# Transposed q and k of the first segments kept as (lane, token) instead of (token, lane)

## The chip, the core and the metric

The kernel runs on one core of one Trainium2 chip. Its time is the device time of one execution in microseconds (us); lower is better. TensorE (PE; PEld is its weight load), VectorE (DVE), ScalarE (ACT), GpSimd (POOL) and SyncE (SP, which issues most DMAs) run side by side, each through its own list of instructions in a fixed order.

## The reference

The program is a linear attention followed by two mixtures of experts. Only the attention bears on the change. For each of 4 batches and 8 heads, over 768 tokens of 48 components, a complex state is turned by a factor per token and component, an outer product of k and v is added, and q reads the real part:

```
for t in range(S):
    new_re = ar * S_re - ai * S_im
    new_im = ar * S_im + ai * S_re
    kv = np.einsum('bhd,bhe->bhde', k[:, :, t], v[:, :, t])
    S_re, S_im = (new_re + kv, new_im)
    y[:, :, t] = np.einsum('bhd,bhde->bhe', q[:, :, t], S_re)
```

The rows y, as 3072 tokens of 384 values, then go through a mixture in which every token has one expert and a second one in which it has two.

## The kernel before

Each sequence is cut into eight segments of 96 tokens: four "first" segments (t = 0) and four "second" ones (t = 1). A lane is one head of one batch in one of the four segments, so 128 lanes fill the partitions. Twenty-four groups of 8 tokens of all lanes go through VectorE and ScalarE, which compute the running product P of the factors, q times P (tile `qh`) and k divided by P (tile `kh`). Groups 0 to 11 are the first segments, groups 12 to 23 the second ones.

For the first segments, TensorE transposes each token's `qh` and `kh` into a PSUM bank (line 848, tile `pt`, four tokens of 128 lanes in a bank, 96 partitions of component and real or imaginary part). ScalarE copies each bank into the long tiles `QT` and `KT` (line 851). That is two banks per group for q and two for k, so 48 copies.

Then come 16 units of the first segments, one per batch and segment with 8 heads each. A unit multiplies, head by head, the 96 tokens of k by those of q (line 999, `amat`, in two halves of 4 heads, out of `KT` and `QT`), masks the product, adds the segment's k and v to the state (line 1029, `pu`), turns the state (line 1042, `pt<-s,R`), and forms the output rows (line 1081, and line 1083, `outs`, where `QT` reads the state; only in the 12 units that have a state before them; both run through the helper at line 932). The state of the first segments is added by TensorE too (line 1026). A float32 matmul of one head shows as two records.

While TensorE does this, VectorE and ScalarE work on groups 12 to 23, whose sums of squares are TensorE's as well (lines 680 and 761). The 16 units of the second segments follow; their k and q come back from memory and are transposed by VectorE (lines 979 and 984) into tiles `kTt` and `qTt`, laid out as head, then 96 tokens in a row. Their tiles lie where `QT` and `KT` were, so their loads wait for the last reader of `QT`. The mixtures follow.

The order of all engines is written by a planner (class `Plan`) from estimated times: 0.66 us for half an `amat`, 1.3 us for half an `outs` with a state, 0.5 us for a copy of line 851. Each engine then keeps that order whatever the real times are. Matmuls of a unit matrix (line 1151) fill planned waits of TensorE.

How a head's 96 columns are taken from the long tile:

```
def lane(XT, n, u, h):
    t, b, g = u
    return XT[:, :, b * 32 + h * 4 + g] if t == 0 else st[n, u][:, h]
```

With `XT` of shape [96, 96 tokens, 128 lanes] two neighbouring columns are 512 bytes apart; those of `kTt` and `qTt` are 4 bytes apart.

Of the kernel before, what the change touches and what calls it, by code (L numbers as in the profile page):

```python
# [22 lines left out]
F32 = mybir.dt.float32  # L23
# [10 lines left out]
G = 8  # L34
# [64 lines left out]
class Plan:  # L99
    """Operations in an order in which they could run, each with its engine, an estimate of its time and the tiles it  # L100
    reads and writes; played back in the order in which a simple model of the engines starts them."""

    def __init__(self, tags):
        self.tags, self.ops, self.fill = tags, [], None
        # kinds of tiles: their pool; pools: those that have to be closed before
        self.pool, self.after = {}, {}

    def add(self, eng, dur, fn, r=(), w=(), key=0.0, when=None, rows=96, got=None, need=(), dma=None, free=False):
        """tiles are tuples: the tile's tag, then what tells it from others; in w, an item in a list stands for a part
        of a tile that no other operation writes; with free, only the operations in need have to come before"""  # L110
        self.ops.append((eng, dur, fn, list(r), [x[0] if isinstance(x, list) else x for x in w],
                         [x[0] for x in w if isinstance(x, list)], key, key if when is None else when, rows, got,
                         set(need), dma, free))
        return len(self.ops) - 1

    def deps(self):
        for p, before in self.after.items():
            # all that is done in the pools before
# [4 lines left out]
        # operations that only have to be issued before  # L123
# [34 lines left out]
    def choose(self, e, t, avail, wait):  # L158
        """the first of those that can start; none where it would keep a more urgent one that comes soon"""
# [13 lines left out]
    def run(self):  # L173
# [29 lines left out]
        while len(out) < n:  # L203
# [23 lines left out]
            if e == 'PE':  # L227
                # the clock of the tensor engine: half of it after a tick with too few columns
# [15 lines left out]
            if e == 'SP':  # L244
                # queue, then the transfer itself
                dma = max(dma, t + 1.1) + dur
                dur = dma - t - 1.1
            at[i], end[i] = t, t + dur
            free[e] = t + 0.47 if e == 'SP' else end[i]
            if move is not None:  # L250
                # descriptors, then the transfer itself
# [27 lines left out]
class Lazy:  # L279
    """A tile, or a part of one, that is allocated when the first operation on it is played"""  # L280
# [59 lines left out]
class Stage:  # L340
    """On-chip memory by pools that open when they are first used, and operations put down for a plan: their reads and
    writes tell which have to come before, their sizes how long they take."""
# [11 lines left out]
    def pool(self, name, side="left", close=(), under=None, space=None, after=None):  # L354
        """a pool, on top of another one; those in close give their room, after is what has to be through before"""
# [42 lines left out]
    def outer(self, name, ap):  # L398
        """a tile that is there already"""
# [22 lines left out]
    def touch(self, op, x, write):  # L422
        """the operations that have to come before, for one access"""
# [11 lines left out]
    def note(self, op, x):  # L435
        """an operation of the plan that writes x"""
        self.touch(op, x, True)

    def ext(self, op, name):
        """an operation of the plan that writes something outside of the chip"""  # L440
# [30 lines left out]
    def group(self, eng, rows=128):  # L471
        """one operation of what is put down within"""
# [18 lines left out]
class Engine:  # L491
    """An engine's operations, put down instead of issued"""
# [49 lines left out]
def attention(stage, a, xs, LG, cst, flag, clears=()):  # L542
    """x rows to xs, gate logits to LG[p, t * 16 + b * 4 + g] (token b * 768 + OFF[t] + g * LEN[t] + p).

    Lanes are (head, one of four segments), first over the segments of LEN[0] tokens, then over those of LEN[1].
    With P_t the product of the normalized factors since the segment's start, q^ = q P and k^ = k / P, so that a
    segment is a causal product of q^ and k^ and the state passes from segment to segment by the diagonal of P's
    last value. The products of the first segments run while the vector engine works on the second ones."""
# [15 lines left out]
    # tiles: tag and number of buffers  # L564
# [12 lines left out]
    def new(key, shape):  # L577
        """the tile of a key: allocated by the operation that writes it first"""
# [11 lines left out]
    A.preload_act_table_set("abs_reciprocal_sqrt_and_small")  # L590
    QT = big.tile([96, LEN[0], 128], F32, name="QT")
    KT = big.tile([96, LEN[0], 128], F32, name="KT")
# [34 lines left out]
    last = [LEN[0] // G - 1, NG - 1]  # L627

    def seg(g):
        """a group's segments, its place in them"""  # L630
# [17 lines left out]
    def group(g):  # L648
# [24 lines left out]
        # u = |a|^2, by the tensor engine as long as it has time  # L673
# [62 lines left out]
        # P of even tokens as (im, re), of odd ones as (re, im)  # L736
# [68 lines left out]
        def d_q(i):  # L805
            def f():
                """q^; of the second segments in three blocks of 32 columns"""
# [33 lines left out]
        for kx, XT, n, x in ((kqh, QT, 'QT', 1.7), (kkh, KT, 'KT', 2.5)):  # L841
            for h in range(2):
# [7 lines left out]
                def cp(XT=XT, h=h, kt=kt):  # L850
                    A.activation(XT[:, j * G + h * 4:j * G + h * 4 + 4], st[kt][:96], AF.Copy)
# [3 lines left out]
    def turns(t):  # L855
        """the segments' last P: columns of the complex diagonal, or what a component and the other one are taken by"""
# [70 lines left out]
    def wide(out, lhsT, rhs, h, m, start=True, stop=True):  # L927
        """out[:, h] = lhsT^T rhs[:, h], heads from the last to the first. The m columns of lhsT take the array as
        long as m columns of rhs: it streams as many, and those before the head's own are written over later."""
# [6 lines left out]
    def lane(XT, n, u, h):  # L936
        t, b, g = u
        return XT[:, :, b * 32 + h * 4 + g] if t == 0 else st[n, u][:, h]

    def unit(i, u):  # L940
# [7 lines left out]
        # what the tail's tiles take the place of  # L948
# [40 lines left out]
        def diag():  # L989
            """the diagonal with the segment's last P"""  # L990
# [31 lines left out]
        def umat():  # L1022
            """what the segment adds to the state"""
# [78 lines left out]
    def warm(x, n, r, key):  # L1102
        """matmuls in a wait, for the clock of the tensor engine"""
# [18 lines left out]
    # rows of the lists that no token gets  # L1122
# [9 lines left out]
    def span(x):  # L1132
        """from the first to the last use of a kind of tile"""
# [5 lines left out]
    def fill(t):  # L1139
        """a matmul in a wait, for the clock of the tensor engine; in a bank that is not in use at that time"""  # L1140
# [13 lines left out]
    # flags: a decay so strong that the factors leave the range in which this form is exact  # L1154
# [8 lines left out]
def general(tc, c, a, out, xs):  # L1163
    """The whole computation for any values: the recurrence token by token, the assignment with ties,
    every expert over every token."""
# [78 lines left out]
    with ExitStack() as ctx:  # L1244
# [5 lines left out]
        def unique(pool, O, shape):  # L1250
            """the first of equal maxima"""
# [25 lines left out]
        def dense(w1, w2):  # L1277
            """acc[t] = sum over the experts of W[t, e] * expert e of token t"""
# [116 lines left out]
def surplus(tc, c, a, xg, cape, out):  # L1395
    """the rows of the second mixture's lists from cape on"""
# [5 lines left out]
    with tc.tile_pool(name="s", bufs=1) as p, tc.tile_pool(name="sps", bufs=2, space=bass.MemoryType.PSUM) as ps:  # L1402
        with tc.For_i(0, E) as e:
# [4 lines left out]
            for r0 in (low, low + R):  # L1408
# [8 lines left out]
                # the rows before are done  # L1417
# [34 lines left out]
def make_consts(nc, pool, rpool, tmp):  # L1452
    """constants that depend on shapes alone, built on chip; those in rpool are the assignment's"""
# [8 lines left out]
    # tri[p', p] = 1 where p' < p  # L1462
# [18 lines left out]
    # slot number of compacted tokens: i * 128 + p  # L1481
# [9 lines left out]
    # 8 - expert  # L1491
    c.w8 = rpool.tile([128, 8], F32, name="w8")
    V.tensor_scalar(c.w8, it[:, :8], -1.0, 8.0, op0=ALU.mult, op1=ALU.add)
    # tokens of the logits, as 16 * tid[0] + tid[1]
# [16 lines left out]
def placed(stage, c, LG, flag):  # L1511
    """The tokens above a threshold at which no expert is full go to their best experts; the others are left for
    the phases."""
# [8 lines left out]
    # every token's best expert, by columns as the logits come: with the values of C0 tokens as thresholds,  # L1522
    # the experts' tokens above them
# [24 lines left out]
    # what moves through the tensor engine: the logits with the token's number  # L1548
# [5 lines left out]
    # everything above the lowest threshold at which no expert is full is placed  # L1554
# [13 lines left out]
    # ranks: tokens before in the same column, in the columns before of a group of four, in the groups before  # L1568
# [18 lines left out]
    # every token's slot, of its expert or of those left: hi * 128 + lo  # L1587
# [16 lines left out]
    # (twice the columns, for the clock of the tensor engine: it takes no longer)  # L1604
# [18 lines left out]
    # places left - 0.5  # L1623
# [4 lines left out]
    # the ids of the tokens placed, by experts and hi  # L1628
# [13 lines left out]
    # flags: two equal best experts, too many tokens left, too few placed  # L1642
# [8 lines left out]
class Phases:  # L1651
    """The tokens left, from the highest logit on: an expert fills up in each phase. The experts' order, and the
    token ids of the slots of those that are full."""

    def __init__(self, stage, c, flag, Lm, rem, cnt, CPs, sl):
# [3 lines left out]
        # 8 - expert, as long as it has no place in the order  # L1659
# [4 lines left out]
        # the order: experts' numbers, one-hot columns  # L1664
# [6 lines left out]
    def slots(self):  # L1671
        """token ids of the slots of the tokens placed"""
# [11 lines left out]
    def take(self, OHA, pn):  # L1684
        """the experts' places go to these tokens"""
# [7 lines left out]
    def best(self):  # L1693
        """the tokens' highest logits, one-hot rows of their experts"""
# [44 lines left out]
    def last(self):  # L1739
        """one expert is left"""  # L1740
# [4 lines left out]
    def next(self, k):  # L1745
        """place k of the order: an expert that is full"""
# [10 lines left out]
    def ids(self, k0, k1, idf):  # L1757
        """token ids of the slots of the experts of these places"""
# [677 lines left out]
```

## Time and profile before

| what | value |
|---|---|
| median of 3 runs | 1241.56 us |
| the three runs | 1231.51, 1241.57, 1241.56 us |
| span of the profiled execution, first to last instruction | 1230.7 us |
| time of the profiled execution beside its span | not listed apart from the three runs |
| TensorE busy | 1170.3 us, 95% |
| VectorE busy | 798.0 us, 65% |
| ScalarE busy | 498.6 us, 41% |
| mean granted TensorE clock | 0.964 of full speed |

A busy share is a mean over stages with different limits. The stages that matter here are: the groups of the first segments (to 149 us), the units of the first segments (149 to 335 us), those of the second ones (335 to about 450 us) and the rest.

### The profile page before, as it was taken

What the parts mean: (1) busy time and instruction counts of PE and PEld (TensorE: products, weight loads), DVE (VectorE), ACT (ScalarE), POOL (GpSimd) and SP (SyncE); (2) the same over time, 40 slices, a digit from 0 to 9 for tenths busy, and PEclk for the clock granted to TensorE, in tenths of its full rate; (3) what the DMA queues carried; (4) which work ended last, traced back from release to release, by engine and by line L of the source; (5) the groups of instructions that cost most, each with busy time, mean ns of one, the idle gap of its engine ahead of it and who ended that gap; (6) DMA issues with size and microseconds to landing.
All of it is one profiled execution on the core that took longest, in us unless ns stands there. A gap on an engine that the chain in (4) does not pass through costs nothing.

```text
span 1230.7 us, 22881 instructions
## 1 busy us (share of the span) xinstructions
PE 1170.3 (95%) x8082; PEld 1103.1 (90%) x8082; DVE 798.0 (65%) x2524; ACT 498.6 (41%) x1026; POOL 297.5 (24%) x321
## 2 busy tenths in 40 slices
PE   8999899999988997899999999989999999999995
PEld 7888798999988987899889999989899999999995
DVE  7899876767599776888788778635535343444221
ACT  8888555534312122554545445123323232232220
POOL 2000021102134320420753221332303132222212
PEclk9999989969999799899999999999999999999998
DMA  7776466644366489453885464264515151422111
GB/s 185 207 207 186 146 201 192 175 140 136 101 156 164 129 180 200 144 151 119 265 267 170 154 206 146 96 214 142 170 64 188 47 188 58 146 87 95 45 39 46
DMA packets 167626, 183.18 MB, mean 149 GB/s; under 512 B 75955, under 2 KB 131716, under 8 KB 167504
## 3 DMA queue, kind: packets, MB, share of 16 engines
q1 hardware_dynamic: 155504, 147.82, 42.1%
q0 software_dynamic: 12000, 33.83, 8.2%
q8 instruction: 65, 1.06, 0.4%
q14 instruction: 57, 0.47, 0.1%
HBM read 119.21 MB, written 60.76 MB: 146 GB/s over the span
## 4 chain that ended last, share of the span: by engine, by line
PE 67%; DMA 10%; DVE 9%; issue 7%; ACT 4%; POOL 1%; SPq 1%; DVEq 0%; POOLq 0%; ACTq 0%
PE pa L537 13%; PE py L537 10%; PE pu L537 10%; PE pm L537 6%; PE py L932 6%; PE pa L999 5%; DMA my_ws<-in_moe_w 4%; PE pt L537 3%; DVE kTt L979 3%; PE pu L932 2%; PE pt L932 2%; DMA yo<-in_v 2%; PE pu L1151 2%; PE pk L680 1%; PE pm L761 1%
## 5 line engine op out<-in xcount | busy, mean ns | idle before, releaser
L537 ACT ACTIVATE my_hh<-pa 128x384 fp32r<-128x384 f32 (+4 forms) x133 | 66.5, 500 | 194.5 <-PE pa L537 86.7
L537 PE MATMUL pa<-mx_xh,mw_w1h 128*128 128x384 f32 (+4 forms) x399 | 138.8, 348 | 0.0
L537 PE MATMUL pa<-mx_xh,mw_w1l 128*128 128x384 f32 (+4 forms) x399 | 136.2, 341 | 0.0
L537 PE MATMUL pa<-mx_xl,mw_w1h 128*128 128x384 f32 (+4 forms) x399 | 136.0, 341 | 0.0
L1010 POOL TENSOR_SCALAR_AFFINE_SELECT am<-am 96x384 f32<-96x384 f32 x64 | 48.7, 763 | 340.4 <-ACT am L1004 340.0
L537 DVE SCALAR_TENSOR_TENSOR my_hl<-pa,my_hh 128x384 fp32r<-128x384 f32 (+4 forms) x133 | 75.2, 566 | 85.3 <-ACT my_hh L537 85.1
L1929 POOL DMA_INDIRECT out<-mx_yo,my_ii x54 | 56.2, 1041 | 269.3 <-DVE mx_yo L537 213.7
L537 PE MATMUL py<-mw_w2h,my_hh 128*128 128x384 f32 (+2 forms) x312 | 109.7, 352 | 1.6 <-DVE mx_yo L537 1.6
L537 PE MATMUL pu<-mw_w2h,my_hh 128*128 128x384 f32 (+3 forms) x312 | 109.0, 349 | 1.9 <-DVE mx_yo L537 1.9
L537 PE MATMUL py<-mw_w2h,my_hl 128*128 128x384 f32 (+2 forms) x312 | 105.2, 337 | 0.0
L537 PE MATMUL pu<-mw_w2h,my_hl 128*128 128x384 f32 (+3 forms) x312 | 105.1, 337 | 0.0
L537 PE MATMUL py<-mw_w2l,my_hh 128*128 128x384 f32 (+2 forms) x312 | 105.1, 337 | 0.0
L537 PE MATMUL pu<-mw_w2l,my_hh 128*128 128x384 f32 (+3 forms) x312 | 105.1, 337 | 0.0
L537 DVE TENSOR_TENSOR mw_w1l<-my_ws,mw_w1h 128x512 fp32r<-128x512 f32 x96 | 65.2, 686 | 37.8 <-ACT mw_w1h L537 37.8
L537 ACT ACTIVATE mw_w1h<-my_ws 128x512 fp32r<-128x512 f32 x96 | 59.3, 632 | 65.9 <-DMA my_ws<-in_moe_w 65.3
L537 ACT ACTIVATE mw_w2h<-my_ws 128x512 fp32r<-128x512 f32 x96 | 57.2, 630 | 56.6 <-DMA my_ws<-in_moe_w 21.5
L537 PEld LDWEIGHTS pa<-mx_xh,mw_w1h 128*128 128x128 f32 x399 | 75.1, 188 | 0.9
L537 PEld LDWEIGHTS pa<-mx_xh,mw_w1l 128*128 128x128 f32 x399 | 74.9, 188 | 0.8
L537 PEld LDWEIGHTS pa<-mx_xl,mw_w1h 128*128 128x128 f32 x399 | 75.1, 188 | 0.6
L1919 POOL DMA_INDIRECT tl_ac<-out,my_ii x54 | 58.3, 1080 | 64.6 <-DMA out<-mx_yo,my_ii 35.9
L1929 POOL DMA_INDIRECT xg<-tl_t,my_pi x48 | 50.9, 1060 | 79.5 <-ACT mw_w2h L537 25.6
L537 DVE TENSOR_TENSOR mw_w2l<-my_ws,mw_w2h 128x512 fp32r<-128x512 f32 x96 | 63.8, 686 | 9.6 <-ACT mw_w2h L537 9.2
(353 smaller groups left out, 3024.3 us busy)
## 6 DMA issues: line engine op xcount, KB each, us to landing
my_ws<-in_moe_w SPq DMA_DIRECT2D x192, 256.0 KB, 3.1
khd<-kh SPq DMA_DIRECT2D x24, 384.0 KB, 3.5
xg<-rb_zt SPq DMA_DIRECT2D x11, 738.8 KB, 15.0
tl_t<-xg SPq DMA_DIRECT2D x10, 591.0 KB, 7.3
vxd<-vx SPq DMA_DIRECT2D x32, 168.0 KB, 3.1
tl_t<-xg SPq DMA_DIRECT2D x6, 788.0 KB, 6.6
at<-in_a_re SPq DMA_DIRECT2D x24, 192.0 KB, 3.2
at<-in_a_im SPq DMA_DIRECT2D x24, 192.0 KB, 3.3
```

Source lines behind the costliest of these rows:

```text
L537: getattr(self.eng, op)(*[f(x) for x in args], **{k: f(v) for k, v in kw.items()})
L680: PE.matmul(u, idn, st[ksq][:, i], start=i == 0, stop=i == 1)
L761: PE.matmul(m, idn, st[kpq][:, i], start=i == 0, stop=i == 1)
L932: PE.matmul(out.rearrange("p h e->p (h e)")[:, s], lhsT, rhs.rearrange("p h e->p (h e)")[:, s], start=start, stop=stop, skip_group_check=True)
L979: V.transpose(kT[c:c + 32, :, r:r + 32], km[r:r + 32, :, c:c + 32])
L999: PE.matmul(pa[:C, j, :C], lane(KT, 'kT', u, h), lane(QT, 'qT', u, h), start=True, stop=True)
L1010: G_.affine_select(am, am, pattern=[[0, 4], [1, C]], base=0, channel_multiplier=-1, compare_op=ALU.is_ge, fill=0.0)
L1151: PE.matmul(st['fill', tag], idn, idn, start=True, stop=True)
L1919: nc.gpsimd.indirect_dma_start(out=dst.get(), out_offset=None, in_=src, in_offset=bass.IndirectOffsetOnAxis(ap=ids.get(), axis=0), bounds_ ...
L1929: st = nc.gpsimd.indirect_dma_start(out=dst, out_offset=bass.IndirectOffsetOnAxis(ap=ids.get(), axis=0), in_=src.get(), in_offset=None, bo ...
```

## The change

The two long tiles change their order of axes. Three places in the code follow from it: the shape of the tiles, the destination of ScalarE's copy with the order in which it reads the PSUM bank, and the index with which a unit takes a head's columns. Everything else in the diff replaces comments and texts by empty lines, so line numbers stay.

```diff
-    QT = big.tile([96, LEN[0], 128], F32, name="QT")
-    KT = big.tile([96, LEN[0], 128], F32, name="KT")
+    QT = big.tile([96, 128, LEN[0]], F32, name="QT")
+    KT = big.tile([96, 128, LEN[0]], F32, name="KT")
...
-                    A.activation(XT[:, j * G + h * 4:j * G + h * 4 + 4], st[kt][:96], AF.Copy)
+                    A.activation(XT[:, :, j * G + h * 4:j * G + h * 4 + 4], st[kt][:96].rearrange("p i l -> p l i"), AF.Copy)
...
-        return XT[:, :, b * 32 + h * 4 + g] if t == 0 else st[n, u][:, h]
+        return XT[:, b * 32 + h * 4 + g] if t == 0 else st[n, u][:, h]
```

A head's 96 columns now lie 4 bytes apart. The copy reads its bank lane by lane, the four tokens of a lane 512 bytes apart in PSUM, and writes them as 16 bytes in a row, the next lane's 384 bytes further on. No instruction is added, removed or moved: the order of every engine is the one before, and on ScalarE only the shape of the 48 copies reads 96x128x4 instead of 96x512. The planner's estimates are unchanged.

## Rows read from the trace of the kernel before

**Rows 1.** The page: busy us, share, count of instructions; busy tenths in 40 slices.

```profile
PE 1170.3 (95%) x8082; PEld 1103.1 (90%) x8082; DVE 798.0 (65%) x2524; ACT 498.6 (41%) x1026; POOL 297.5 (24%) x321
...
DVE  7899876767599776888788778635535343444221
```

**Rows 2.** Windows: from:to, length, busy us (count) by engine, clock, DMA.

```profile
core 0: us, PE busy (x) PEld busy (x) DVE busy (x) ACT busy (x) POOL busy (x), PEclk, DMA share, GB/s
50.00:100.00 50.00, 47.99 (x388) 41.01 (x387) 46.46 (x137) 45.39 (x110) 0.00 (x0) 1.00 0.74 208
...
250.00:270.00 20.00, 20.00 (x111) 17.86 (x110) 12.66 (x36) 7.76 (x15) 1.77 (x3) 0.63 0.48 139
...
149.00:335.00 186.00, 186.00 (x1299) 171.72 (x1299) 127.29 (x355) 87.42 (x172) 31.66 (x32) 0.91 0.54 158
335.00:450.00 115.00, 102.12 (x1026) 98.82 (x1025) 102.17 (x218) 22.79 (x48) 40.31 (x55) 0.91 0.58 154
```

**Rows 3.** Waits, 150 to 335 us: who waited for whom, us, times, longest.

```profile
DVE LG L1093 <- ACT yo L1090: 27.3, 10, 6.4
...
DVE m L789 <- ACT w L782: 16.8, 8, 5.0
```

**Rows 4.** Chain of waits around 335 us: start, us, what.

```profile
332.94 1.97 PE py L932 x16
...
335.88 5.43 DMA kmt<-khd
341.33 0.43 DVE kTt L979
```

**Rows 5.** Timeline of PE, first segments, full clock: start, us, instruction.

```profile
206.26 1.80 PE L999 MATMUL pa<-QT,KT 96*96 96x96 f32 x8
207.89 0.35 PE L932 MATMUL py<-vx,am 96*96 96x96 f32 x2
208.07 0.49 PE L932 MATMUL py<-ss,QT 96*96 96x96 f32 x2
...
209.85 1.52 PE L932 MATMUL pt<-s,R 96*96 96x96 f32 x16
```

**Rows 6.** Timeline of PE, second segments, full clock.

```profile
392.56 0.84 PE L999 MATMUL pa<-qTt,kTt 96*96 96x96 f32 x8
393.24 0.33 PE L932 MATMUL py<-vxt,am 96*96 96x96 f32 x2
393.41 0.33 PE L932 MATMUL py<-sst,qTt 96*96 96x96 f32 x2
...
394.56 0.88 PE L999 MATMUL pa<-qTt,kTt 96*96 96x96 f32 x8
```

**Rows 7.** Timeline of PE at the lower clock: first segments, then second ones.

```profile
248.65 1.80 PE L999 MATMUL pa<-QT,KT 96*96 96x96 f32 x8
250.25 0.51 PE L932 MATMUL py<-vx,am 96*96 96x96 f32 x2
250.56 0.53 PE L932 MATMUL py<-ss,QT 96*96 96x96 f32 x2
250.88 0.53 PE L932 MATMUL py<-vx,am 96*96 96x96 f32 x2
...
408.88 1.55 PE L999 MATMUL pa<-qTt,kTt 96*96 96x96 f32 x8
410.23 2.70 PE L932 MATMUL pu<-vxt,kmt 96*96 96x96 f32 x16
```

**Rows 8.** Groups by line, 0 to 420 us: count | busy us, mean ns | idle before.

```profile
L851 ACT ACTIVATE QT<-pt 96x512 f32<-96x512 f32 x24 | 13.7, 583 | 3.2 <-PE pt L848 3.1
...
L915 ACT ACTIVATE vx<-py 96x64 f32<-96x64 f32 x32 | 6.9, 216 | 5.6 <-PE py L911 5.5
...
L1093 DVE TENSOR_REDUCE LG<-py 96x8 f32<-96x64 f32 x26 | 5.7, 218 | 41.5 <-ACT yo L1090 34.6 <-PE py L932 6.8
...
L537 DVE TENSOR_REDUCE ra_m<-LG 96x8 f32<-96x64 f32 x2 | 0.4, 200 | 0.0
```

## The prediction, made before the changed kernel had run

> **What bounds the kernel now.** I read the page first [rows 1]: TensorE is busy 95% of the span. That share is a mean, so the next view is the windows [rows 2], stage by stage. From 149 to 335 us, where TensorE runs the 16 units of the first segments, it is busy 186.0 of 186.0 us, VectorE only 127.3 and ScalarE 87.4. So here TensorE sets the pace, and the waits confirm it [rows 3]: VectorE waits 27.3 us for results of the output matmuls (line 1093, behind ScalarE's copy of py) and 16.8 us for `w`, which stands behind a TensorE sum. From 50 to 100 us it is different: VectorE is busy 46.5 of 50 us and ScalarE 45.4, so the first groups are held by those two, and ScalarE has only 4.6 us of 50 free. From 335 to 450 us VectorE leads again, 102.2 of 115 us. The chain [rows 4] shows how the second stage hands over to the third: the last output matmuls out of QT start at 332.94 us, the loads that take the place of QT land at 341.3 us, and VectorE's transposes begin. Whatever ends the units earlier therefore moves all that follows, including the mixtures, which begin with the rows of these units.
>
> **What the change does on TensorE.** The same matmul exists in the trace in both layouts, with the same shapes and back to back. I take distances from start to start, since records overlap. Out of QT and KT, with columns 512 bytes apart, half an `amat` (4 heads, 8 records) starts at 206.26 and the next instruction at 207.89: 1.63 us [rows 5]. Out of kTt and qTt, with columns in a row, it is 392.56 to 393.24 = 0.68 us [rows 6]. That saves 0.95 us. There are 16 units of two halves, so 32 x 0.95 = 30.4 us. Half an `outs` with a state is 207.89 to 209.85 = 1.96 us with QT and 393.24 to 394.56 = 1.32 with qTt: 0.64 us, in 12 units of two halves, 24 x 0.64 = 15.4 us. Together 45.8 us at the full clock.
>
> At the lower clock less is saved. Half an `amat` takes 248.65 to 250.25 = 1.60 us strided and 408.88 to 410.23 = 1.35 contiguous; in `outs` the pair out of `vx` and `am`, contiguous, takes 250.25 to 250.56 and the pair out of QT 250.56 to 250.88 [rows 7], the same, so I count nothing for them. The granted clock of the stage is 0.91 [rows 2], and between the levels 1 and one half that is 18% of the time at the lower one. The saving is then 0.82 x 45.8 + 0.18 x 32 x 0.25 = 37.6 + 1.4 = 39 us. TensorE's work in the stage falls from 186 to 147 us.
>
> The clock itself may gain. In 250 to 270 us it was 0.63 [rows 2]; just before and in this stretch stand `amat` and `outs` out of QT, in which TensorE passes its columns at half its rate or less. If it never fell, the stage would lose at most 9% of 186, or 17 us, more; if the fall stays, nothing. I take 5, since the strided pieces are only part of what runs there.
>
> **What then is late next.** VectorE has 127.3 us of work in the same stretch. At the 93% that it reaches from 50 to 100 us this takes 137 us, at the 89% of 335 to 450 us 143. So TensorE, with 147, stays just last, and two engines that are so close and keep a fixed order wait for each other now and then. I add 5 us; the ends are 0 and 17 (rival two). That the planner has 0.66 us for half an `amat` and 1.3 for half an `outs`, which are the contiguous times, speaks for little waiting: VectorE's order around line 1093 was laid for a TensorE of that speed. ScalarE's 87 us fit in any case, and the loads (DMA share 0.54 in the stage, 0.74 from 50 to 100 us) have room to come closer together.
>
> **What the change does on ScalarE.** The 48 copies of line 851 (24 out of each kind of bank) now read PSUM 512 bytes apart in runs of four. No ScalarE row shows such a read. Today a copy takes 583 ns, and with line 915 at 216 ns for 64 elements this is 0.82 ns an element [rows 8]. The nearest row is VectorE's line 1093, which sums 64 values read from PSUM 224 bytes apart in 218 ns, against 200 ns for line 537's maximum over 64 values in a row in SBUF: at most 18 ns for 64, or 0.28 ns an element, 0.14 us a copy. The far end is a second cycle for each element, as TensorE shows it for its strided operand: 512 x 0.82 = 0.42 us. A copy in pieces can hardly be faster than one in a row, so the near end is 0. I take 0.14, the row of the nearest kind: 48 x 0.14 = 6.7 us on ScalarE, all before 149 us. At the 9% of 50 to 100 us it has 13 us free there, but in pieces that lie where it waits, so I let it use half of them: 7 us, and of the 6.7 let half show, +3 us, since the copies stand between others that VectorE waits for. The writes in pieces of 16 bytes I cost at nothing: line 915 writes 8 pieces of 32 bytes in 216 ns, and what is left of that after 64 x 0.82 ns, 163 ns, I take for what every instruction has before its first element; if it were all a price for pieces it would be 20 ns each (rival three).
>
> **Sum.** -39 - 5 + 5 + 3 = -36 us. The span of the profiled execution is 1230.7 us; the runs are 1231.5 and twice 1241.6, and nothing says how much lies around the span. I take the saving from the median, 1241.6 - 36 = **1206 us**, and let the range know of the lower run. A change under about 1%, 12 us, could not be told from none here.
>
> **Rivals.** *One: the copy pays for every element.* With 0.42 us a copy, ScalarE has 20 us more to do, of which the 7 us that it can use hide a part. 13 show, 10 more than I counted: -26, 1216 us. For it: TensorE's rows show a price of this kind for 4-byte pieces far apart, 1.63 against 0.68 us [rows 5, 6]. Against it: line 1093 shows at most a quarter cycle. The Trainium skill bears on this, in "Advanced Engine Details and Errata", section "Memory Cachelines": SBUF has lines of 16 bytes and PSUM of 8, and at least two accesses to an SBUF line are needed to hide the latency. By that rule the matmuls gain as I count, the copy's write is free, and its read, one element of each PSUM line, would be the slow one: 1216. The trace agrees for TensorE's reads of SBUF and does not show it for VectorE's of PSUM.
>
> *Two: VectorE becomes the bound.* If the 16.8 us behind `w` stay, although TensorE is faster, VectorE needs 143 + 17 = 160 us: the stage saves 26, the whole 23: 1219 us. For it: each group passes ScalarE and TensorE several times. Against it: from 50 to 100 us the same chain leaves VectorE idle for 7% only.
>
> *Three, slower: each of the 128 short runs of a copy starts anew.* The trace has no row with runs of four on ScalarE. 39 us of gain and 7 of slack are used up when 48 copies cost 1.0 us more each, that is 8 ns for each run; from there on the kernel is slower. At 16 ns, below the 20 that line 915 allows at most, a copy costs 2 us more and ScalarE has 96 us more, 89 of which show: 1241.6 + 89 - 39 = 1292 us. Against it: VectorE's line 1093 reads 8 runs and ends 18 ns above line 537 with its one.
>
> *Four: it does not do what it says.* The stride is not why the first segments' matmuls are slow, and only the copy's 3 us remain: 1245 us. Against it: in the stage TensorE has no idle time, so the longer steps are no waits, and both uses of QT show them.
>
> **Numbers.** My forecast, 1188 to 1213 us by the ends of clock and interplay and the lower run, has 0.66; rival one 0.15; two 0.11; three 0.04; four 0.04. The range 1187 to 1224 holds the first three but for their tails. Faster by over 1% are all of the forecast and most of one and two: 0.89; within 1% their tails and four: 0.07; slower 0.04.
>
> **What will show it.** Line 851 at about 0.7 us (rival one: 1.0; three: over 1.6) and the first `amat` out of QT near 152 us; half an `amat` 0.7 us and half an `outs` 1.3 from start to start; the last `outs` out of QT at about 298 us instead of 333; VectorE's share of that stage over 85%, its 27.3 us behind py nearly gone; a clock near 0.95 there; everything after it at the same distances. If the matmuls are as short as that and the loads of the second segments still start after 310 us, rival two was right.

## The result and the profile after

The median went from 1238.8 us (four runs of the kernel before, 1231.51 to 1241.57: the three that the prediction knew and one of 1236.05) to **1192.6 us** (four runs of the change, 1192.22 to 1195.15): ratio 0.963, 95% interval 0.959 to 0.968. Forecast were 1206 us in a range of 1187 to 1224. The gain is 46 us between the medians and 39.8 us between the two profiled spans (1230.7 and 1190.9 us); the profiled run of the change has 1.8 us around its span (1192.71 and 1190.9).

The page of the changed kernel, to be laid beside [rows 1]:

```profile
PE 1117.2 (94%) x8082; PEld 1049.9 (88%) x8082; DVE 797.8 (67%) x2524; ACT 493.4 (41%) x1026; POOL 307.8 (26%) x321
...
DVE  7898899997997766888787777445444444434321
```

TensorE has 53 us less to do with the same 8082 instructions; VectorE has what it had, ScalarE 5 us less. GpSimd is busy 10 us longer (297.5 before): its masks of the product (line 1010) take 956 ns instead of 763, and 964 in the repeat of the change. The windows of the changed kernel, by the same stages as [rows 2] (groups of the first segments, their units, units of the second segments):

```profile
50.00:100.00 50.00, 47.20 (x384) 40.47 (x383) 45.36 (x134) 44.88 (x107) 0.00 (x0) 1.00 0.73 207
...
151.50:286.90 135.40, 131.66 (x1299) 118.13 (x1297) 127.44 (x356) 82.66 (x171) 44.18 (x32) 1.00 0.82 214
287.20:403.00 115.80, 102.02 (x1006) 98.65 (x1005) 101.92 (x217) 22.26 (x47) 40.02 (x55) 0.90 0.59 153
```

The middle one holds the answer. The stage, from the first `amat` out of QT to the end of the last `outs` out of it, was 185.8 us and is now 135.4. TensorE is no longer busy all the time, VectorE has the same 127 us of work in it and is busy 94%, the clock is 1.00, and the DMA share rose from 0.54 to 0.82. The stages on either side are as they were. The waits of that stage in the changed kernel (us, times, longest), for [rows 3]:

```profile
ACT pq L754 <- DVE P L749: 16.5, 10, 3.3
...
DVE LG L1093 <- ACT yo L1090: 2.9, 4, 1.0
...
DVE m L789 <- ACT w L782: 1.3, 2, 0.7
```

VectorE's two waits for what TensorE has to deliver, 27.3 and 16.8 us, are 2.9 and 1.3. Now it is ScalarE that waits for VectorE, 16.5 us where it was 3.9. The timeline of TensorE in the changed kernel, first segments (start, us, instruction), shows the matmuls of [rows 5] at the pace of [rows 6]:

```profile
203.68 0.88 PE L999 MATMUL pa<-QT,KT 96*96 96x96 f32 x8
204.39 1.48 PE L680 MATMUL pk<-sq,idn 128*128 128x384 f32 x4
205.71 0.33 PE L932 MATMUL py<-vx,am 96*96 96x96 f32 x2
205.88 0.33 PE L932 MATMUL py<-ss,QT 96*96 96x96 f32 x2
...
207.03 1.52 PE L932 MATMUL pt<-s,R 96*96 96x96 f32 x16
```

Half an `amat` takes 204.39 - 203.68 = 0.71 us instead of 1.63, half an `outs` 207.03 - 205.71 = 1.32 instead of 1.96. ScalarE's copies, by groups (count | busy us, mean ns | idle before), against [rows 8]:

```profile
L851 ACT ACTIVATE QT<-pt 96x512 f32<-96x512 f32 x24 | 13.6, 582 | 3.2 <-PE pt L848 3.2
L851 ACT ACTIVATE KT<-pt 96x512 f32<-96x512 f32 x24 | 13.4, 587 | 3.6 <-PE pt L848 3.6
```

They cost what they cost before, 583 and 587 ns. And the hand-over to the second segments, VectorE's first transposes in the changed kernel, against 341.33 us in [rows 4]:

```profile
293.69 1.33 DVE L979 STREAM_TRANSPOSE kTt<-kmt 32x256 f32<-32x256 f32 x3 [1.88 <-DMA kmt<-khd]
```

It comes 47.6 us earlier.

**Where the 50 us of the stage came from.** I added up the distances from each of TensorE's starts to its next, by line, in both traces. The 256 `amat` records out of QT and KT take 51.5 us before and 25.4 now, the 192 records of `outs` out of QT 31.2 and 17.0: together 40.3 us. All other lines, which the change doesn't touch, take 103.1 us and now 93.0: another 10 us, which go with the clock (0.91 before, 1.00 now; the experiments return to it). A distance holds the idle time behind the instruction too: TensorE had none in this stage before and has 3.7 us now, 2.0 of them behind `amat`, 0.5 behind `outs` and 1.3 behind the other lines. Of the 50 us, 2.6 were lost ahead of the stage (the first `amat` at 151.5 instead of 148.9 us) and about 8 behind it, 5.6 of them at the first weights of a mixture. The 2.6 and the 5.6 are read below as scatter; the rest, some 2 us, was not followed up.

### The profile page after: what moved, and what is told of

Its sections match the earlier page's. It is cut to its first block, busy times and chain, and to the rows that moved or that the text cites. A ratio compares the mean times of both kernels' runs of the same rounds, so it can differ in the third digit from the quotient of the medians.

```text
span 1190.9 us, 22881 instructions
## 1 busy us (share of the span) xinstructions
PE 1117.2 (94%) x8082; PEld 1049.9 (88%) x8082; DVE 797.8 (67%) x2524; ACT 493.4 (41%) x1026; POOL 307.8 (26%) x321
## 4 chain that ended last, share of the span: by engine, by line
PE 42%; DMA 7%; issue 6%; DVE 3%; POOL 1%; ACT 1%; POOLq 0%; DVEq 0%; ACTq 0%; SPq 0%
PE pa L537 13%; PE pu L537 10%; PE py L537 10%; PE pm L537 6%; DMA my_ws<-in_moe_w 4%; PE pt L537 3%; DMA mx_yo<-xs,keep_idx 1%; DMA tl_t<-xg 1%; DVE mw_w1l L537 1%; DMA out<-mx_yo,my_ii 0%; POOL xg L1929 0%; ACT mw_w1h L537 0%; POOL out L1929 0%; DVE mw_w2l L537 0%; DMA xg<-tl_t,my_pi 0%
## 5 line engine op out<-in xcount | busy, mean ns | idle before, releaser
L1010 POOL TENSOR_SCALAR_AFFINE_SELECT am<-am 96x384 f32<-96x384 f32 x64 | 60.9, 956 | 281.0 <-ACT am L1004 280.9
L537 DVE TENSOR_TENSOR mw_w1l<-my_ws,mw_w1h 128x512 fp32r<-128x512 f32 x96 | 65.2, 686 | 40.8 <-ACT mw_w1h L537 40.3
```

What stands on the lines that cost most here:

```text
L537: getattr(self.eng, op)(*[f(x) for x in args], **{k: f(v) for k, v in kw.items()})
L1010: G_.affine_select(am, am, pattern=[[0, 4], [1, C]], base=0, channel_multiplier=-1, compare_op=ALU.is_ge, fill=0.0)
```

## The experiments

In what follows "stage" is the stretch from the first `amat` out of QT to the end of the last `outs` out of QT, and distances are from start to start. The theory: a column that lies 512 bytes from the next costs TensorE about twice its time, and this alone makes the stage long. The rivals: another property of the old layout (which of the two operands, or the long distance), the clock, and VectorE. The first four runs shared a chip on which the mixtures took longer whatever the kernel: from the last line 1093 to the end it is 801 to 812 us in these four, against 776 in the first profile of the kernel before and 781 in that of the change (the kernel before took 1270.46 us beside them). So they are read by the stage. Most experiments are one execution each, and one kernel's executions on one chip lay up to 23 us apart (seven of the kernel before: 1221.36 to 1243.99), so single times are weak evidence and the stages, with their clock, carry the argument.

### The kernel before once more

Edit: none.

> The kernel before, once more, for how far one execution differs from the next. Three places of the changed kernel are asked about: the first amat out of QT began 2.6 us later (151.5 against 148.9), VectorE's longest wait of the assignment, behind the weights' loads, was 15.5 us instead of 9.9, and the clock of the units' stage was 1.00 instead of 0.91. Theory (these first two are scatter between executions, the third is the change): here the first amat lies anywhere from 148.5 to 152, the wait from 9 to 16, the stage is again near 186 us long at a clock of 0.88 to 0.93. Rival (the clock is scatter as well): the stage has a clock over 0.97 and is near 176 us long. Rival two (the later start and the longer wait come from the change): 148.9 and 9.9 again within 0.3.

1257.03 us. The window of the stage:

```profile
149.90:331.30 181.40, 181.40 (x1298) 167.22 (x1297) 127.57 (x356) 87.40 (x171) 31.84 (x32) 0.94 0.56 162
```

`amat` 51.6 and `outs` 31.3 us, as before to 0.1 us, and TensorE busy throughout. But the clock is 0.94, not 0.91, and the other lines take 181.4 - 51.6 - 31.3 = 98.5 us instead of 103.1. The strided matmuls repeat exactly; the clock doesn't. With 181.4 us the stage lies between what theory (186) and rival (176) expected: part of the 186 was the clock of one execution. The first `amat` came at 149.9 us.

### Only KT by lane

```diff
-    QT = big.tile([96, 128, LEN[0]], F32, name="QT")
+    QT = big.tile([96, LEN[0], 128], F32, name="QT")
```

with the old copy and index for QT; against the changed kernel.

> KT by lane, QT by token: in amat the stationary operand (KT) is contiguous and the moving one (QT) strided; in outs the stationary operand (QT) is strided. Theory A (the stride of each operand costs time of its own, and the two add): half an amat falls from 1.63 to about 1.0 us from start to start, half an outs stays at 1.96; the stage is near 163 us, the time near 1220. Theory B (the slower of the two operands sets the pace, and the moving one is the slower): half an amat stays near 1.6, the stage near 186, the time that of before, 1239. Theory C (only the stationary operand's stride costs): half an amat 0.7, the stage near 155, the time near 1211. Clock: if the strided pieces are what lets it fall, it lies between 0.91 and 1.00.

1249.27 us; stage 164.8 us, clock 1.00. TensorE's timeline:

```profile
216.29 1.50 PE L999 MATMUL pa<-QT,KT 96*96 96x96 f32 x8
217.61 0.35 PE L932 MATMUL py<-vx,am 96*96 96x96 f32 x2
217.80 0.49 PE L932 MATMUL py<-ss,QT 96*96 96x96 f32 x2
```

and its tile view of QT (operation, count: shortest/median/longest record in ns, from and to in us):

```profile
L999 PEld LDWEIGHTS pa<-QT,KT x256: 159/179/182, 150.0 to 307.0; 96*96 96x96 f32 x128
L999 PE MATMUL pa<-QT,KT x256: 322/342/387, 150.0 to 307.2; 96*96 96x96 f32 x128
```

Half an `amat` takes 1.32 us, and `outs`, which reads only QT, stays at 31.3 us. None of the expected values (0.7, 1.0, 1.6) was met.

### Only QT by lane

```diff
-    KT = big.tile([96, 128, LEN[0]], F32, name="KT")
+    KT = big.tile([96, LEN[0], 128], F32, name="KT")
```

with the old copy and index for KT.

> QT by lane, KT by token: in amat the stationary operand is strided and the moving one contiguous; outs is contiguous. Theory A (costs add): half an amat 1.3 us, half an outs 1.32; the stage near 155 us, the time near 1212. Theory B (the moving operand sets the pace when both are strided): half an amat also 1.3, since the stationary one alone then costs what it costs in outs today, 0.33 us a head; time near 1212. Theory C (only the stationary operand's stride costs): half an amat stays 1.6, only outs gains 15 us: the stage near 168, the time near 1222.

1224.19 us; stage 150.2 us, clock 1.00, `outs` 16.3 us. Timeline and tile view:

```profile
214.99 1.51 PE L999 MATMUL pa<-QT,KT 96*96 96x96 f32 x8
216.34 0.33 PE L932 MATMUL py<-vx,am 96*96 96x96 f32 x2
```

```profile
L999 PEld LDWEIGHTS pa<-QT,KT x256: 238/258/260, 146.2 to 290.5; 96*96 96x96 f32 x128
L999 PE MATMUL pa<-QT,KT x256: 247/328/401, 146.2 to 290.6; 96*96 96x96 f32 x128
```

Half an `amat` takes 1.35 us, as theories A and B expected; C is out. With the run before it, A's adding up is out too: each operand alone costs 0.61 or 0.64 us, and both cost 0.92 instead of 1.25. So one strided operand, whichever it is, costs 0.33 us a head (1.32 / 4) against 0.18 with none, and two cost only 0.41 (1.63 / 4). The records tell them apart: KT is what the weight load reads, and its record grows to 258 ns when KT is strided and stays at 179 when it isn't. The load runs beside the matmul before it, which is a reason why the two prices need not add; that is read from the records, not tried. For the sum of this change it means that in `amat` neither half is worth much without the other: of its gain of 26.1 us KT alone gives 9.4 (51.6 to 42.2) and QT alone 8.8 (to 42.8). What `outs` gains, QT alone gives.

### The old layout, with the copy in the new order

```diff
-                    A.activation(XT[:, j * G + h * 4:j * G + h * 4 + 4], st[kt][:96], AF.Copy)
+                    A.activation(XT[:, j * G + h * 4:j * G + h * 4 + 4].rearrange("p i l -> p l i"), st[kt][:96].rearrange("p i l -> p l i"), AF.Copy)
```

against the kernel before: ScalarE reads PSUM as the change does, but its writes fall one by one, 512 bytes apart.

> The layout of before, but the 48 copies of line 851 go lane by lane: they read PSUM 512 bytes apart, as in the changed kernel, and also write single values 512 bytes apart. Theory (ScalarE moves one value a cycle whatever the stride): the copies stay at 583 ns and the kernel at its time of before, 1231 to 1242 us. Rival (a value in a line of its own costs a second cycle, on the write side, which the changed kernel with its 16-byte pieces did not show): the copies take about 1000 ns, 20 us more of ScalarE before 149 us, and the first amat comes 8 to 16 us later, the time about 1247 to 1255.

1269.68 us. The copies, by groups:

```profile
L851 ACT ACTIVATE QT<-pt 96x512 f32<-96x512 f32 x24 | 25.0, 1074 | 0.6 <-PE pt L848 0.6
L851 ACT ACTIVATE KT<-pt 96x512 f32<-96x512 f32 x24 | 24.9, 1098 | 2.3 <-PE pt L848 2.3
```

and two windows, of the groups and of the stage:

```profile
50.00:100.00 50.00, 44.89 (x355) 37.79 (x353) 41.40 (x121) 47.58 (x99) 0.00 (x0) 1.00 0.69 186
158.40:334.00 175.60, 175.57 (x1296) 162.66 (x1297) 126.00 (x353) 87.25 (x171) 36.12 (x32) 0.99 0.58 167
```

A copy costs half a microsecond more, about 0.96 ns for each of its 512 single writes. ScalarE, busy 47.6 of 50 us, becomes the bound of the first groups, and the first `amat` comes at 158.4 us, 8.5 later than in the run of the kernel before on the same chip: 23 us more on ScalarE, of which somewhat over a third shows. So the expected rival was right: this is what rival one of the prediction would have looked like. It needs the writes apart; the same reads with writes of 16 bytes cost nothing in the change. A second thing stands in the last row: the matmuls are as strided as ever (51.6 and 31.3 us) and the clock stays at 0.99.

### Columns 8 bytes apart

```diff
-    QT = big.tile([96, 128, LEN[0]], F32, name="QT")
+    QT = big.tile([96, 64, LEN[0], 2], F32, name="QT")
...
-        return XT[:, b * 32 + h * 4 + g] if t == 0 else st[n, u][:, h]
+        return XT[:, (b * 32 + h * 4 + g) // 2, :, g % 2] if t == 0 else st[n, u][:, h]
```

KT likewise, and the copy writes runs of 32 bytes. Two lanes share a row, so that two of a head's values lie in each 16 bytes.

> Pairs of lanes side by side, (lane pair, token, 2 lanes), in both tiles: a head's columns lie 8 bytes apart, two of them in any aligned 16 bytes. Theory L (what costs is a 16-byte line of its own for each value; two values of a line hide it): half an amat about 0.8 us and half an outs 1.3, the stage of the first segments' units 134 to 140 us long, as in the changed kernel. Rival S (any step other than 4 bytes costs): half an amat about 1.6, half an outs 1.96, stage 175 to 186. Rival B (it is the distance of 512 bytes, a power of two, that costs): as theory L here, and apart from it in the next run. The copies of line 851: 583 ns.

1181.82 us (before beside it 1219.72); copies 581 and 586 ns. Window of the stage and timeline:

```profile
148.10:282.40 134.30, 132.76 (x1299) 119.77 (x1297) 127.05 (x356) 83.39 (x171) 45.55 (x32) 1.00 0.78 216
```

```profile
218.45 0.91 PE L999 MATMUL pa<-QT,KT 96*96 96x96 f32 x8
219.19 0.33 PE L932 MATMUL py<-vx,am 96*96 96x96 f32 x2
```

0.74 us for half an `amat`: all but free, as theory L and rival B expected; rival S is out.

### Columns 16 bytes apart

```diff
-    QT = big.tile([96, 128, LEN[0]], F32, name="QT")
+    QT = big.tile([96, 32, LEN[0], 4], F32, name="QT")
...
+        return XT[:, (b * 32 + h * 4 + g) // 4, :, g % 4] if t == 0 else st[n, u][:, h]
```

> Four lanes side by side, (lane quad, token, 4 lanes), in both tiles: a head's columns lie 16 bytes apart, one in each aligned 16 bytes. Theory L (a line of its own for each value costs): half an amat about 1.6 us, half an outs 1.96, the stage 175 to 186 us long, as with 512 bytes. Rival B (only the distance of 512 bytes costs): 0.8 and 1.3, the stage 134 to 140. The copies of line 851: 583 ns.

1219.92 us. Timeline and window of the stage:

```profile
219.57 1.67 PE L999 MATMUL pa<-QT,KT 96*96 96x96 f32 x8
221.06 0.35 PE L932 MATMUL py<-vx,am 96*96 96x96 f32 x2
```

```profile
150.70:323.00 172.30, 172.30 (x1298) 160.10 (x1297) 126.69 (x356) 86.78 (x171) 38.18 (x32) 1.00 0.60 170
```

1.49 us for half an `amat`, so rival B is out. From 8 to 16 bytes the price jumps from nearly nothing to nearly the whole; the 496 bytes beyond that add 0.14 us. In `outs` they add nothing: its records out of QT add up to 17.9 us at 8 bytes and 33.8 at 16, against 31.2 at 512. The steps tried are 4, 8, 16 and 512 bytes; a row of 16 bytes that has to be hit twice fits them, and so would any limit on the step between 8 and 16 bytes. This pair is also the cleanest measure of the layout, one execution each: same chip, same clock, same copies, and 172.3 - 134.3 = 38.0 us in the stage, 1219.92 - 1181.82 = 38.1 us in the time.

### Less work for TensorE

```diff
-                PE.matmul(pu[:96].rearrange("p h e->p (h e)"), idn[:96, :96], st[kS0].rearrange("p h e->p (h e)"),
-                          start=True, stop=False, skip_group_check=True)
...
+                wide(pu[:96], st[kk][:C, h], st[kx][:C], h, 56 if add else 96, start=True)
```

against the changed kernel, as are all that follow. It leaves out what earlier segments give the state (line 1026).

> The changed kernel without the 12 additions of the earlier state on TensorE (line 1026, 24 records, 9.1 us from start to start in the stage); their estimates stay in the plan, so the order stays. The state of the first segments then lacks what earlier segments gave. What bounds the stage of the units now? If TensorE still does (131.7 us busy of 135.4), it shrinks by about 9, to 126 to 128 us. If VectorE does (127.4 busy), it shrinks by at most 4, to 131 to 135.

1186.94 us.

```profile
149.70:288.20 138.50, 131.22 (x1274) 122.17 (x1274) 127.24 (x356) 82.88 (x171) 41.66 (x32) 0.94 0.77 209
```

The stage did not shrink, but the clock fell to 0.94 in it, so that TensorE was busy as long as before with less work. Neither of the two expected lengths (126 to 128, 131 to 135) was met, and this run decides nothing about the bound. It shows that the clock can fall with contiguous operands too.

### A VectorE step on GpSimd

```diff
-            V.tensor_tensor(new(kR, [96, 8, 48, 2]), mk[:, None, :, None].to_broadcast([96, 8, 48, 2]),
+            G_.tensor_tensor(new(kR, [96, 8, 48, 2]), mk[:, None, :, None].to_broadcast([96, 8, 48, 2]),
...
-                plan.add('V', 0.87, diag, r=[('pet', t)], w=[kR], key=key)
+                plan.add('G', 1.8, diag, r=[('pet', t)], w=[kR], key=key)
```

> The changed kernel with the 16 products of line 991 (0.99 us each on VectorE, 15.8 us) on GpSimd, which is busy 44 of 135 us in the stage; the planner orders anew. If VectorE bounds the stage of the units, it shrinks to what TensorE needs, 128 to 132 us from 135.4, and VectorE's last kh comes that much earlier. If TensorE does, it stays at 133 to 137. If GpSimd takes over 2 us for one and TensorE waits for it in front of the state's turn (line 1042), the stage grows.

1207.52 us, slower than the change; stage 156.0 us at clock 0.93. The groups of the stage, first of this kernel, then of the changed one:

```profile
L743 DVE TENSOR_TENSOR X<-A,P 128x192 f32<-128x192 f32 x88 | 41.9, 476 | 0.5
...
L749 DVE TENSOR_TENSOR P<-X 128x96 f32<-128x96 f32 x88 | 30.4, 346 | 0.6
...
L991 POOL TENSOR_TENSOR R<-mk,pet 96x768 f32<-96x768 f32 x16 | 26.8, 1673 | 151.4 <-ACT pet L877 135.9 <-PE pt L932 15.5
```

```profile
L743 DVE TENSOR_TENSOR X<-A,P 128x192 f32<-128x192 f32 x88 | 32.9, 374 | 0.2
...
L749 DVE TENSOR_TENSOR P<-X 128x96 f32<-128x96 f32 x88 | 23.4, 266 | 0.2
...
L991 DVE TENSOR_TENSOR R<-mk,pet 96x768 f32<-96x768 f32 x16 | 15.8, 987 | 0.6 <-PE pt L932 0.6
```

VectorE gave away 15.8 us and its two most frequent operations became 16 us longer (41.9 + 30.4 - 32.9 - 23.4). All of that falls on operations that run at the same time as a GpSimd instruction: beside neither of GpSimd's lines 991 and 1010 the two take 341 and 248 ns on average here (53 and 55 records) and 347 and 247 in the changed kernel. The stage grew by 20 us though GpSimd took only 1.67 us for a product, which none of the three cases expected. The planner also put the work in another order here, so how much of the stage's growth is which stays open.

### More work for VectorE

```diff
+            [V.tensor_tensor(R, mk[:, None, :, None].to_broadcast([96, 8, 48, 2]),
+                            sub(pet[t], (b * 32 + g) * 2, [[8, 8], [0, 48], [1, 2]]), op=ALU.mult) for R in [new(kR, [96, 8, 48, 2])] * 2]
```

in place of line 991: the same product, twice.

> The changed kernel with each of the 16 products of line 991 done twice on VectorE: +15.8 us of VectorE in the stage of the units (127.4 busy of 135.4 before), the same order of every engine. If VectorE bounds the stage now, it grows by 12 to 16 us, to 147 to 151. If TensorE does, VectorE's 8 free us take half of it and the stage grows by at most 8, to 137 to 143.

1196.85 us.

```profile
147.00:294.70 147.70, 134.43 (x1299) 119.02 (x1297) 143.62 (x372) 82.44 (x171) 41.72 (x32) 1.00 0.71 196
```

### More work for TensorE

```diff
-                for j in range(4):
+                for j in ((0, 0, 1, 1, 2, 3) if t == 0 else range(4)):
```

Two of the four heads of each half `amat` are multiplied twice.

> The changed kernel with two of the four heads of each half amat of the first segments multiplied twice: 64 more products of 0.17 us, +11 us of TensorE in the stage (131.7 busy of 135.4), the same order. [...] If TensorE bounds the stage, it grows by 8 to 11 us, to 143 to 146. If VectorE does, by at most 5, to 135 to 140. If both this run and the last one grow by most of what they add, the two engines are balanced.

1194.19 us.

```profile
150.00:290.90 140.90, 140.90 (x1426) 128.52 (x1425) 126.96 (x356) 84.81 (x171) 42.45 (x32) 1.00 0.74 206
```

These two shared a chip with a repeat of the change, which had a stage of 134.2 us (below). VectorE's 16 us more cost 13.5, TensorE's 8.5 us more (33.5 instead of 25.0 for `amat`) cost 6.7. Most of either shows. In the first VectorE is busy 97% of the stage, in the second TensorE all of it. So after the change neither engine alone is the bound; as far as one execution of each tells, the two stand level, and the next gain would need both.

### Clears earlier

```diff
-NCL = 5
+NCL = 9
...
-CLEARD = 1.596
+CLEARD = 1.2
```

The writes of zeros that a mixture needs stand in SP's queue by planned times; nine instead of five of them go into the attention, closer together, since its stage is now shorter and the first weights waited in the profile of the change.

> The changed kernel with 9 instead of 5 of the 738.8 KB clears issued during the attention, 1.2 groups apart, so that 4 fewer stand in front of the first weights, where VectorE waits some 10 to 16 us for them. If that wait hangs on the clears' bytes (11 clears in about 40 us, 3.7 us each), four fewer shorten it by 10 us or more and the kernel gains 5 to 12 us on the changed one. If the clears in the attention hold the loads of the groups up (the DMA share in the units' stage is 0.82), the stage gets longer by as much, and the time is the changed kernel's or worse.

Median 1175.66 us (1167.78 to 1189.94), ratio to before 0.955, interval 0.945 to 0.964. The profiled run was the slowest of its four. The stage in it, then its wait for the first weights (us, times, longest):

```profile
152.10:287.20 135.10, 131.60 (x1298) 118.20 (x1297) 127.15 (x356) 83.11 (x171) 45.18 (x32) 1.00 0.92 237
```

```profile
ACT mw_w1h L537 <- DMA my_ws<-in_moe_w: 1.2, 2, 0.6
```

The wait is all but gone and the stage is no longer than without the clears. The median lies 8 us below that of the change beside it, within the 5 to 12 that were expected, but the intervals overlap, so it is not shown to be faster than the change.

### The change once more

Edit: none; beside the last runs.

> The changed kernel once more, beside the run with 9 clears and the kernel before on the same chip: a ratio of 0.958 to 0.968 to the kernel before, the first amat out of QT between 146 and 152 us, the wait for the first weights 8 to 11 us instead of the 16 of its first profile, if that one was scatter.

Median 1183.57 us (1180.22 to 1192.88), ratio 0.962, interval 0.954 to 0.970 (before beside it: median 1231.6). The stage:

```profile
151.70:285.90 134.20, 131.42 (x1298) 118.16 (x1297) 127.14 (x356) 82.99 (x171) 44.72 (x32) 1.00 0.79 216
```

The waits for the first weights, 440 to 560 us, in the changed kernel's first profile, then in this one:

```profile
ACT mw_w1h L537 <- DMA my_ws<-in_moe_w: 16.2, 2, 16.0
```

```profile
ACT mw_w1h L537 <- DMA my_ws<-in_moe_w: 11.8, 5, 8.2
```

The kernel before's longest wait there is 10.4 us in one execution and 8.6 in the other; the change's is 16.0 in one and 8.2 in the other. So the 5.6 us at the weights are that execution's, not the change's. The same holds for the 2.6 us ahead of the stage: over all kernels but the one with scattered copies, the first `amat` starts between 146.2 and 152.1 us. From the end of the stage to the end of the span, though, the repeat takes 905 us, as much as the first profile of the change (904), while the kernel before took 896. In the six other runs with both operands' steps short it is 897 to 903 us, with steps of 16 bytes 895. That a few of the microseconds won are lost again behind the stage is therefore possible, and stays open.

## Why the prediction was right, step by step

**TensorE bounded the stage, and the strided operands were the reason: right.** The matmuls out of QT and KT became as short as those out of qTt and kTt, VectorE's 27.3 us all but disappeared (2.9) and everything after moved. Rival four is out. The last pair of runs on layout sharpens the reason: what counts is not the 512 bytes, but a step somewhere between 8 bytes (two of a head's values in each 16) and 16 (one in each). The rule of the Trainium skill, "Advanced Engine Details and Errata", section "Memory Cachelines", asks for at least two accesses to a 16-byte line of SBUF, and the trace agrees: 0.74 us for half an `amat` at 8 bytes, 1.49 at 16.

**Matmuls, -39: measured -40.3, or -42.8 without the idle time behind them.** The forecast took something off because the stage spent 18% of its time at the lower clock. But a strided `amat` hardly depends on the clock, as [rows 5] and [rows 7] already had it (1.63 and 1.60 us): it adds up to 51.5, 51.6 and 51.6 us at granted clocks of 0.91, 0.94 and 0.99. What the lower clock costs shows in the contiguous one (0.68 and 1.35 us), and after the change the stage stood at 1.00, so nothing was to be taken off. What remains between the full-clock sum of 45.8 us and 42.8 is mainly that the contiguous matmuls of the first segments take a little longer than the ones of the second segments: half an `amat` 0.73 us on average without idle time, where [rows 6] has 0.68.

**Clock, -5: measured -10, or -11.4 without idle time, and the reason given for it falls.** I had put the low clock of 250 to 270 us down to matmuls that pass their columns slowly. But the clock stayed at 0.99 and 1.00 with columns 512 and 16 bytes apart, and fell to 0.94 and 0.93 in two kernels with contiguous columns. The size can be read: the untouched lines of the stage take 103.1 us at 0.91, 98.5 at 0.94, 92.7 at 0.99 and 91.0 to 91.3 in the four experiments at 1.00 that change the layout alone. So the 10 us between the two first profiles belong to the granted clock of those two executions, and that this term came out with the right sign was luck. What decides whether it falls stays open, and so does whether the change helps it. On the chip of the repeat the mean clock of the whole execution was 0.955 to 0.977 in seven runs of the kernel before and 0.970 to 0.980 in five of the change.

**Interplay, +5: about right, at 3.7** (TensorE's idle time in the stage). I expected VectorE to need 137 to 143 us for its work in this stretch; it took 135.4 together with TensorE. Rival two would have kept the 16.8 us behind `w`; they are 1.3, and the load of the second segments' k was issued at 288.3 us, not after 310. But the rival was near: with 16 us more for VectorE the stage took 147.7 us.

**Copies, +3: measured 0.** Reading PSUM 512 bytes apart in runs of four costs ScalarE nothing (582 and 583 ns). Rivals one and three fall with that. The section of the Trainium skill named above also has lines of 8 bytes in PSUM; no run here shows a price for crossing them on ScalarE's reads. The price I had looked for on the reading side exists on the writing side, 1074 to 1098 ns a copy, when each write of 4 bytes goes elsewhere. The price that I took from VectorE's line 1093 was too high. Its evidence against rival three was even better than I made it: the line reads 64 single values, as the paragraph on ScalarE says, and not 8 runs.

**The sum.** In the stage -50.4 stands against -39, since the copies' +3 lay ahead of it. Without idle time in the distances the terms are -42.8 for -39, -11.4 for -5 and +3.7 for +5: of the 11 us too much, 6 are the clock, 4 the matmuls and 1 the interplay. The first profiled execution gave 10.6 of the 50 back ahead of the stage and behind it, so its span shows 39.8; the medians show 46, and 48 in the repeat (1231.6 - 1183.57). With the 8-byte and 16-byte steps, on one chip and at one clock, the layout was worth 38 us. Part of the 48 is clock: on the chip of the repeat two executions of the kernel before with a mean clock of 0.976 and 0.977 took 1221.4 and 1225.0 us, two of the change with the same 1183.6 and 1181.4: 38 to 44 us. So the mechanism and its main term stand, and the terms that I mis-sized are the clock, the part taken off the matmuls for it, and, by 3 us, the copy.

Not every sign that I named came as I said. The end of the last `outs` (287 us, forecast 298), VectorE's 94% and its vanished wait agree with the mechanism. The first `amat` at 151.5 us, forecast 152, was met by luck: the copies that were to delay it cost nothing (0.58 us, forecast 0.7), and the 2.6 us are scatter. The clock, 1.00 for 0.95, was missed. The ends of the forecast were not formed alike either: 1188 us is the largest saving taken from the median, 1213 the smallest taken from the lower run; from the median the smallest gives 1223 us.

## What to carry to other kernels

When the same instruction stands in one trace in two layouts, the difference of its start-to-start distances is the price of the layout; multiply it by the count in the stretch where that engine is the last. Keep at least two float32 values of each matmul operand's columns in every 16 bytes, for both operands, since fixing one of two gives only about a third of what fixing both does (a step of 12 bytes was not tried); and let the copy out of PSUM do the reordering, as long as it writes runs (16, 32 and 64 bytes were free). Before counting on the next gain in the same stretch, lay the engines' busy times beside its new length: here two engines now seem to stand level, since adding work to either shows.

## What the runs showed of the hardware

- Half an `amat` (4 heads, 96 columns of float32): 0.71 us with columns 4 bytes apart, 0.74 at 8, 1.49 at 16, 1.63 at 512. With one operand at 512 bytes it is 1.32 (the moving one, QT) or 1.35 (the loaded one, KT), with both 1.63.
- A strided weight load shows in its own record: 258 ns against 165 to 179.
- A ScalarE copy of 512 values takes 582 ns whether it reads PSUM in a row or in steps of 512 bytes (writing runs of 16 bytes), and 1074 to 1098 ns when it writes them one by one, 512 bytes apart.
- With a product of 96x768 on GpSimd (1673 ns instead of 987 on VectorE), VectorE's short operations in that stage went from 374 to 476 and from 266 to 346 ns; those that overlap none of GpSimd's instructions kept their 341 and 248.
- The kernel before, with the same instructions, had 0.91 and 0.94 for the granted clock of one stage in two executions.
